# Holding expert weights back, rearranging the filling chain and adding filler matmuls in a fused attention and expert-routing kernel

## The chip, the cores and the metric

The kernel runs on one core of one Trainium2 chip. The metric is device time in microseconds of one execution, lower being better; the median of three runs of the kernel before is 372.67 us (371.42 to 376.82). The core has a matrix engine (TensorE, PE in the profile, with its weight loads as PEld), a vector engine (DVE), a scalar engine (ACT), GpSimd (POOL), a sync engine (SP) and 16 DMA engines that all queues share. Each engine takes its instructions in order and waits on semaphores.

## The reference

Two operators follow each other. The first is a linear attention with decay over q, k, v of shape (4, 8, 768, 64), in blocks of 64 positions; the second sends each of the 3072 resulting tokens (512 features) to one of eight experts, each with room for exactly 384 tokens, and applies that expert's two-layer network. The inputs are float32. Cut to what matters:

```python
for b in range(nb):                                  # blocks of one sequence
    intra = einsum('bhic,bhjc->bhij', qb, kb) * Dmask
    intra = einsum('bhij,bhjd->bhid', intra, vb)
    inter = einsum('bhid,bhde->bhie', qb * lam_pow, kv_state)
    out[:, :, sl] = intra + inter
    kv_state = lam_block * kv_state + einsum('bhsd,bhse->bhde', kb_dec, vb)

x = attn_out.transpose(0, 2, 1, 3).reshape(3072, 512)
logits = x @ w_gate                                  # 3072 x 8
order = argsort(-logits.flatten())                   # greedy, best pair first
for idx in order:
    tok, e = idx // E, idx % E
    if assigned[tok] >= 0 or counts[e] >= cap: continue    # cap = 384
    assigned[tok] = e; counts[e] += 1
for e in range(E):
    h = maximum(x[assigned == e] @ w1[e], 0.0)       # 512 -> 1024
    out[assigned == e] = h @ w2[e]                   # 1024 -> 512
```

The routing is sequential in the reference: an expert that fills up sends its later candidates to their next choice. The kernel finds the point at which each expert fills by counting.

## The kernel before

**Attention** (`_Attn`, run at L1070). 24 groups of 128 tokens pass through a software pipeline. In step s the loop loads group s + 3 (L909: q, k and v, 256 KB each, on SP's queue), turns q and k of group s + 1 on PE, applies the scores of group s - 1 to its values, computes the router's logits of group s - 2 (`gate`, L1055, whose copy at L1068 fills `logits[:, s - 2]`), computes the scores of group s (ACT and DVE split them into two bf16 parts, POOL masks them with an affine select at L979), and stores the attention output of group s - 1 to `x_dram` (L1043, 256 KB, on SP's queue). After that `hook(s)` runs, which also issues router constants, the ranges of the logits and the loads of expert weights 0 to 3 in steps 21 to 24 (L1136). A weight is one of sixteen matrices, w1 and w2 of eight experts in turn, read as float32 and written as bf16, 1 MB in SBUF. Load m is `load_w(m)` at L530, on POOL's queue. Weights 0 to 9 have their own room from the start. This part of the program is ordered on each engine by the framework's planner, which takes instructions as their inputs become ready and not strictly as they are written.

**Routing and experts** (`_route_and_moe`, L612). From here the order on PE, POOL and DVE is the written one. `router.phase1` is a generator. Its `first` (L200) settles the expert that fills first: three rounds, each of 24 matmuls that count tokens above thresholds (L222; the first at L228 and L230), a comparison and a one-matmul sum (`settle`, L205). Then it computes the positions of that expert's tokens and of the tokens that are first choices, builds one-hot matrices and, in 24 matmuls (L286), the token numbers `perm0` of the first two experts' first 256 tokens. 24 more matmuls (`psC`, L303) compact the tokens that are left over into 5 columns. Six filling steps (`steps`, L364) follow; each has three rounds of 5 counting matmuls (L388), one summing matmul (L404) and DVE work between them. In the first round of the first step `rest` (L328) also computes `R24`, `psT` (24 matmuls, L339) and with it `perm1`, the first 256 tokens of all experts. `perm2`, the last 128 tokens of each expert, comes after step 6.

Sixteen expert jobs run on PE: jobs 0 to 7 take 256 tokens of each expert, jobs 8 to 15 the last 128. A job gathers rows of `x_dram` by token number (L550, on POOL's queue, 128 rows at a time), turns them (L564), multiplies by w1 (`up`, L581), applies the maximum on ACT (L586), multiplies by w2 (`down`, L594), copies the result on ACT (L599, four buffers `oe`) and scatters it by token number to the output (L600, on POOL's queue). The filling steps are woven into the jobs' matmuls: a small planner keeps an estimate t of PE's time, each piece of a job adds its cost, and a filling step yields the delay in `WAIT` (L474) after which its next matmuls are to be put into PE's order. Loads 4 to 8 are written behind `moe.open` (L1141), load 9 behind the first gathers that need `perm1` (L668), and after the `up` of each job two more loads (L645), ahead of that job's two scatters.

## Time and profile before

| what | value |
|---|---|
| median of three runs | 372.67 us (371.42 to 376.82) |
| the profiled execution's own time | 374.97 us |
| its span, first to last instruction | 373.2 us |
| mean granted clock of PE | 0.82 |
| busy: PE, DVE, ACT, POOL | 268.0, 185.6, 168.2, 161.6 us |
| DMA queue of POOL / of SP and others by hardware | 26.22 MB, 37.7% / 25.19 MB, 31.9% of 16 engines' span |
| result scatters (L600) | 24, first issued at 242.5 us, last at 365.3 us |

Times in the profile are microseconds from the start of the span, unless marked ns. A line of the timeline names start, length, engine, source line, operation, output and inputs, and in brackets how long the engine sat idle before it and what released it. A release that names an engine long done hides another wait, often a DMA. SPq and POOLq are the queues' own entries: DMA issues and waits on semaphores. In the waits, columns are total, number of times and the longest. A DMA share above 1 means that packets on one engine overlap. The granted clock is a share of PE's full speed.

### The profile page before, as it was taken

What the parts mean: (1) busy time and instruction counts of PE and PEld (TensorE: products, weight loads), DVE (VectorE), ACT (ScalarE), POOL (GpSimd) and SP (SyncE); (2) the same over time, 40 slices, a digit from 0 to 9 for tenths busy, and PEclk for the clock granted to TensorE, in tenths of its full rate; (3) what the DMA queues carried; (4) which work ended last, traced back from release to release, by engine and by line L of the source; (5) the groups of instructions that cost most, each with busy time, mean ns of one, the idle gap of its engine ahead of it and who ended that gap; (6) DMA issues with size and microseconds to landing.
All of it is one profiled execution on the core that took longest, in us unless ns stands there. A gap on an engine that the chain in (4) does not pass through costs nothing. (4 is left out here: it accounts for less than half of the span.)

```text
span 373.2 us, 8812 instructions
## 1 busy us (share of the span) xinstructions
PE 268.0 (72%) x3551; PEld 210.7 (56%) x3551; DVE 185.6 (50%) x587; ACT 168.2 (45%) x297; POOL 161.6 (43%) x189
## 2 busy tenths in 40 slices
PE   2778455649588887988885556999939099786990
PEld 2567344528477786877764444666725067453760
DVE  3666505236467887788977655576716043000000
ACT  4655405345476786777620001444421236452650
POOL 5976322516355656557326044216060352535521
PEclk9998865685689899899965555799978679996997
DMA  8999999999996886874110042995939442414421
GB/s 155 218 181 213 216 218 212 177 209 218 220 224 156 189 205 145 190 175 112 61 53 5 2 56 33 188 205 104 205 73 186 99 102 82 100 59 117 95 86 35
DMA packets 96976, 52.05 MB, mean 139 GB/s; under 512 B 76960, under 2 KB 88224, under 8 KB 96928
## 3 DMA queue, kind: packets, MB, share of 16 engines
q0 software_dynamic: 17920, 26.22, 37.7%
q1 hardware_dynamic: 79008, 25.19, 31.9%
q8 instruction: 30, 0.49, 0.5%
q14 instruction: 18, 0.15, 0.1%
HBM read 58.74 MB, written 12.58 MB: 191 GB/s over the span
## 5 line engine op out<-in xcount | busy, mean ns | idle before, releaser
L581 PE MATMUL p<-xeT,w 128*128 128x256 bf16 (+1 forms) x512 | 53.9, 262 | 17.7 <-ACT hT L586 16.4
L600 POOL DMA_INDIRECT out_dram<-oe,perm x24 | 24.3, 1014 | 81.0 <-ACT oe L599 49.6
L581 PEld LDWEIGHTS <-w 128*128 128x128 bf16 x512 | 42.0, 103 | 27.6 <-issue 19.3
L979 POOL TENSOR_SCALAR_AFFINE_SELECT sp<-sp 128x512 f32<-128x512 f32 x48 | 30.7, 646 | 61.7 <-DVE sp L976 57.6
L594 PE MATMUL p<-w,hT 128*128 128x512 bf16 x192 | 47.5, 392 | 0.0
L975 ACT CAST sp<-S 128x512 bf16<-128x512 f32 x48 | 32.2, 738 | 22.0 <-PE S L970 21.9
L586 ACT ACTIVATE hT<-p 128x512 bf16<-128x512 f32 (+1 forms) x64 | 31.1, 491 | 22.4 <-PE p L581 16.6
L976 DVE TENSOR_TENSOR sp<-S,sp 128x512 bf16<-128x512 f32 x48 | 32.9, 734 | 15.4 <-ACT sp L975 15.2
L1010 PE MATMUL XL<-vh,sp 128*128 128x64 bf16 x384 | 27.7, 208 | 12.8 <-POOL sp L979 12.5
L550 POOL DMA_INDIRECT xe<-x_dram,perm x24 | 25.2, 1050 | 25.2 <-DVE B L294 11.2
L599 ACT COPY oe<-p 128x512 f32<-128x512 f32 x24 | 14.1, 586 | 46.2 <-DMA out_dram<-oe,perm 22.8
L933 POOL TENSOR_TENSOR vl<-vs,vh 128x512 bf16<-128x512 f32 x24 | 28.6, 1192 | 13.4 <-ACT vh L931 13.1
L1010 PEld LDWEIGHTS <-sp 128*128 128x128 bf16 x576 | 24.5, 108 | 16.3 <-POOL sp L979 14.9
L928 POOL TENSOR_TENSOR vs<-vf,lamneg 128x512 f32<-128x512 f32 x24 | 25.8, 1074 | 17.0 <-DMA vf<-in_v_dram 13.3
L568 ACT COPY xeT<-pt 128x1024 bf16<-128x1024 bf16 (+1 forms) x16 | 12.8, 798 | 42.9 <-PE pt L564 42.7
L925 ACT CAST kp<-kf 128x512 f16<-128x512 f32 x24 | 18.9, 789 | 27.6 <-DMA kf<-in_k_dram 27.6
L926 DVE TENSOR_TENSOR kp<-kf,kp 128x512 f16<-128x512 f32 x24 | 19.6, 816 | 23.4 <-ACT kp L925 23.4
L970 PE MATMUL S<-qh,kT 64*128 64x128 f16 x384 | 30.1, 239 | 1.2 <-DVE sp L976 1.1
L942 PE MATMUL kT_ps<-identf,kp 128*128 128x128 f32 x96 | 19.3, 338 | 15.8 <-DVE kp L926 11.0
L594 PEld LDWEIGHTS <-hT 128*128 128x128 bf16 x192 | 17.7, 100 | 17.9 <-issue 1.8
L970 PEld LDWEIGHTS <-kT 64*128 64x128 f16 x576 | 20.9, 104 | 10.3 <-issue 6.9
L1029 PE MATMUL stp<-vh,kp 128*128 128x128 bf16 x160 | 22.0, 252 | 4.7 <-ACT vh L931 3.9
(257 smaller groups left out, 592.7 us busy)
## 6 DMA issues: line engine op xcount, KB each, us to landing
w<-in_moe_w_dram POOLq DMA_DIRECT2D x16, 1024.0 KB
qf<-in_q_dram SPq DMA_DIRECT2D x24, 256.0 KB, 4.6
kf<-in_k_dram SPq DMA_DIRECT2D x24, 256.0 KB, 5.2
vf<-in_v_dram SPq DMA_DIRECT2D x24, 256.0 KB, 5.3
x_dram<-xs SPq DMA_DIRECT2D x24, 256.0 KB, 2.8
xe<-x_dram,perm POOLq DMA_INDIRECT x24
out_dram<-oe,perm POOLq DMA_INDIRECT x24
lam_sb<-in_lam_dram SPq DMA_DIRECT2D x1, 4.0 KB, 2.6
```

The costliest lines, as they stand in the source:

```text
L550: nc.gpsimd.indirect_dma_start(out=xe[:, c, :], out_offset=None, in_=self.x_dram, in_offset=bass.IndirectOffsetOnAxis(ap=pm, axis=0), boun ...
L581: nc.tensor.matmul(p1[:, f, 0:n, :], self.w1t[e][:, kc, fc * P : (fc + 1) * P], j["xeT"][:, kc, 0:n, :], start=(kc == 0), stop=(kc == 3), ...
L586: nc.scalar.activation(hT[:, fp, :, 0:n, :], p1[:, :, 0:n, :], ACT.Relu)
L594: nc.tensor.matmul(p2, j["hT"][:, kc // 2, kc % 2, c, :], self.w2t[e][:, kc, :], start=(kc == 0), stop=(kc == 7))
L600: nc.gpsimd.indirect_dma_start(out=self.out, out_offset=bass.IndirectOffsetOnAxis(ap=j["perms"][c], axis=0), in_=oe, in_offset=None, bound ...
L928: nc.gpsimd.tensor_tensor(vs, vf, self.lamneg[:, t, :, None].to_broadcast([P, 8, 64]), OP.mult)
L933: nc.gpsimd.tensor_tensor(vl, vs, vh, OP.subtract)
L970: nc.tensor.matmul(S[a][:, hp, :], kT[r, hp, :, ks], qq[r, hp, :], start=(i == 0), stop=(i == 2))
L975: nc.scalar.copy(s[:, :, :, 1], S[a])
L976: nc.vector.tensor_tensor(s[:, :, :, 0], S[a], s[:, :, :, 1], OP.subtract)
L979: nc.gpsimd.affine_select(out=sf, in_=sf, compare_op=OP.is_ge, fill=0.0, base=0, pattern=[[0, 4], [1, P]], channel_multiplier=-1)
L1010: nc.tensor.matmul(X[a][:, hp, :], sp[a][:, hp, :, ss], vv[:, h, :], start=(first and hp == 0 and i == 0), stop=(i == 2), skip_group_check ...
```

## The change

Seven edits, in the words of the code:

- `load_w` takes `after`: it first copies one logit on DVE into the first element of the weight tile, which the load then overwrites. Loads 0 to 6 are issued in steps 18 to 24 with the logits of group s - 2; loads 7 and 8 stay behind `moe.open` and have no such copy.
- Load 9 follows the first gathers, loads 10 and 11 follow the gathers of jobs 2 and 3 once `perm1` is there, and each later job issues one load ahead of its first scatter and one behind it. Gathers run four jobs ahead instead of three.
- `R24`, `psT` and `tok1` move from `rest` into `first`, behind `psC`.
- The filling step keeps the expert scores of dead tokens and masks the maximum instead; what the next step does not need at once moves behind its first indicators (`settled`).
- `warm(us)` issues `int(us / 0.11)` matmuls of 256 columns into an unused PSUM tile; it is called in `settle`, in `count`, before the last count of the first round, before `perm0`'s matmuls and before `psC`.
- `WAIT` has other values; the third, used once, goes from 1.5 to 5.5.
- `phase1` is given the tile for `warm`.

```diff
         G.tensor_tensor(self.zp[:, :, 1, a:b], Z, H, OP.add)
-    def phase1(self, ctx, L):
+    def warm(self, us):
+        for _ in range(int(us / 0.11) if self.spare is not None else 0):
+            self.nc.tensor.matmul(self.spare, self.identb,
+                                  self.i_kt.rearrange("p k t -> p (k t)")[:, 0:256],
+                                  start=True, stop=True)
+    def phase1(self, ctx, L, spare=None):
         tc = self.tc
...
         self.ps = ps
+        self.spare = spare
         self.sp2 = ctx.enter_context(tc.tile_pool(name="r2", bufs=2))
...
             nps = ps.tile([P, 8], F32, tag="n")
+            self.warm(0.25)
             nc.tensor.matmul(nps, onesm, S, start=True, stop=True)
...
                                 self.i_kt[:, 0:64, ts], OP.is_ge)
+                self.warm((0.9, 0.35)[hh])
                 for t in range(hh * 12, hh * 12 + 12):
...
         self.ranks(L, 23, 24)
+        self.warm(0.6)
         nc.tensor.matmul(cps, self.ind23, ohb[:, 23, :], start=False, stop=True)
...
         pe1 = ps.tile([P, 2, 6], F32, tag="n")
+        self.warm(3.0)
         for t in range(24):
...
         psC = ps.tile([P, 18, 5], F32, tag="pos")
+        self.warm(1.2)
         for t in range(24):
...
                              start=(t == 0), stop=(t == 23))
+        R24 = sp.tile([P, 2, 24, 24], F16, name="R24")
+        V.tensor_tensor(R24[:, 1], self.i_j[:, 0:24, :],
+                        jb[:, None, :].to_broadcast([P, 24, 24]), OP.is_equal)
+        V.tensor_tensor(R24[:, 0], R24[:, 1], self.i_t, OP.mult)
+        V.tensor_scalar(R24[:, 1], R24[:, 1], self.i_p, None, OP.mult)
         c1 = st.tile([P, 8], F32, name="c1")
...
         self.nf, self.big = nf, big
+        psT = ps.tile([P, 2, 24], F32, tag="cnt")
+        for t in range(24):
+            nc.tensor.matmul(psT.rearrange("p a j -> p (a j)"), A[:, :, t],
+                             R24[:, :, :, t].rearrange("p a j -> p (a j)"),
+                             start=(t == 0), stop=(t == 23))
         Z = st.tile([P, 8, 5], F32, name="Z")
...
         self.occ, self.alive = occ, alive
+        tok1 = st.tile([P, 8, 3], F32, name="tok1")
+        V.reduce_sum(tok1.rearrange("p e j -> p (e j)"), psT.rearrange("p a j -> p j a"), axis=AX.X)
+        self.tok1 = tok1
         def rest():
...
             self.tp = tp
-            R24 = sp.tile([P, 3, 24, 24], F16, tag="R", name="R24")
-            V.tensor_tensor(R24[:, 2], self.i_j[:, 0:24, :],
-                            jb[:, None, :].to_broadcast([P, 24, 24]), OP.is_equal)
-            V.tensor_tensor(R24[:, 0], R24[:, 2], self.i_t, OP.mult)
-            V.tensor_scalar(R24[:, 1], R24[:, 2], self.i_p, None, OP.mult)
-            psT = ps.tile([P, 2, 24], F32, tag="pos")
-            for t in range(24):
-                nc.tensor.matmul(psT.rearrange("p a j -> p (a j)"), A[:, :, t],
-                                 R24[:, 0:2, :, t].rearrange("p a j -> p (a j)"),
-                                 start=(t == 0), stop=(t == 23))
-            tok1 = st.tile([P, 8, 3], F32, name="tok1")
-            V.reduce_sum(tok1.rearrange("p e j -> p (e j)"), psT.rearrange("p a j -> p j a"),
-                         axis=AX.X)
-            self.tok1 = tok1
             perm1 = st.tile([P, 8, 3], I32, name="perm1")
...
         Z, alive, nf, big = self.Z, self.alive, self.nf, self.big
-        eoh = ge = oh = None
+        zr = nm = nps = am = oh = None
+        def settled(zr, nm, nps, am):
+            eoh = sp.tile([P, 8], F32, tag="eoh")
+            V.tensor_scalar(eoh, nps, nm, None, OP.is_equal)
+            V.scalar_tensor_tensor(big, eoh, 1.0e6, big, OP.mult, OP.add)
+            ge = sp.tile([P, 5], F32, tag="ge")
+            V.tensor_scalar(ge, zr, nm, None, OP.is_ge)
+            ga = sp.tile([P, 5], F32, tag="ga")
+            V.tensor_tensor(ga, ge, am, OP.mult)
+            V.tensor_tensor(self.aoi, self.aoi, ga, OP.add)
+            return ge
         for i in range(1, 7):
+            zm = sp.tile([P, 5], F32, tag="zm")
+            V.reduce_max(zm, Z, axis=AX.X)
             z = sp.tile([P, 5], F32, tag="z")
-            V.reduce_max(z, Z, axis=AX.X)
+            V.tensor_tensor(z, zm, alive, OP.mult)
             poh, oh = oh, sp.tile([P, 5, 8], BF16, tag="oh")
-            V.tensor_tensor(oh, Z, z[:, :, None].to_broadcast([P, 5, 8]), OP.is_equal)
-            zr = z
+            pzr, pnm, pnps, pam, zr = zr, nm, nps, am, z
             for r in range(3):
...
                     V.tensor_scalar(ind[:, c, :], self.kvec[r], zr[:, c : c + 1], None, OP.is_le)
+                if r == 0:
+                    V.tensor_tensor(oh, Z, zm[:, :, None].to_broadcast([P, 5, 8]), OP.is_equal)
                 if r == 0 and i > 1:
+                    ge = settled(pzr, pnm, pnps, pam)
                     ao = sp.tile([P, 5, 8], BF16, tag="ao")
...
                     yield rest()
+            V.scalar_tensor_tensor(nf, nps, nm, nf, OP.not_equal, OP.mult)
             V.scalar_tensor_tensor(alive, zr, nm, alive, OP.is_lt, OP.mult)
-            eoh = sp.tile([P, 8], F32, tag="eoh")
-            V.tensor_scalar(eoh, nps, nm, None, OP.is_equal)
-            V.tensor_tensor(nf, nf, eoh, OP.subtract)
             if i < 6:
-                V.tensor_tensor(Z, Z, alive[:, :, None].to_broadcast([P, 5, 8]), OP.mult)
                 V.tensor_tensor(Z, Z, nf[:, None, :].to_broadcast([P, 5, 8]), OP.mult)
-            V.scalar_tensor_tensor(big, eoh, 1.0e6, big, OP.mult, OP.add)
-            ge = sp.tile([P, 5], F32, tag="ge")
-            V.tensor_scalar(ge, zr, nm, None, OP.is_ge)
-            ga = sp.tile([P, 5], F32, tag="ga")
-            V.scalar_tensor_tensor(ga, zr, nm, am, OP.is_ge, OP.mult)
-            V.tensor_tensor(self.aoi, self.aoi, ga, OP.add)
+        ge = settled(zr, nm, nps, am)
         ef = sp.tile([P, 1], F32, tag="ef")
...
         yield perm2
-    WAIT = (1.5, 2.5, 1.5, 0.55, 2.2, 1.6)
+    WAIT = (1.4, 2.3, 5.5, 0.35, 2.2, 1.6)
     def flag(self):
...
             self.w2t[e] = pool.tile([128, 8, 512], BF16, name=f"w2_{e}")
-    def load_w(self, m):
+    def load_w(self, m, after=None):
         e = m // 2
-        if m % 2 == 0:
-            self.nc.gpsimd.dma_start(out=self.w1t[e], in_=self.w1r[e])
-        else:
-            self.nc.gpsimd.dma_start(out=self.w2t[e], in_=self.w2r[e])
+        w, src = (self.w2t[e], self.w2r[e]) if m % 2 else (self.w1t[e], self.w1r[e])
+        if after is not None:
+            self.nc.vector.tensor_copy(w[0:1, 0, 0:1], after)
+        self.nc.gpsimd.dma_start(out=w, in_=src)
     def open(self, ctx):
...
         self.mps = ctx.enter_context(tc.tile_pool(name="mps", bufs=2, space=bass.MemoryType.PSUM))
+    def spare(self):
+        return self.mps.tile([128, 256], F32, tag="p1", name="spare")
     def gather(self, perms):
...
     with tc.manual_schedule(engines={E.PE, E.Pool, E.DVE}):
-        gen = router.phase1(ctx, L)
+        gen = router.phase1(ctx, L, moe.spare())
         jobs = [None] * 16
...
         later = list(later)
+        moe.load_w(later.pop(0))
         perm1 = perm2 = None
...
                     yield from moe.turn(jobs[n + 1])
-                if jobs[min(n + 3, 15)] is None:
-                    ahead(n + 3)
-                for _ in range(2):
-                    if later:
-                        moe.load_w(later.pop(0))
+                if jobs[min(n + 4, 15)] is None:
+                    ahead(n + 4)
+                if later:
+                    moe.load_w(later.pop(0))
                 for c in range(len(jobs[n]["perms"])):
                     yield from moe.down(jobs[n], n % 8, c)
+                    if later and c == 0:
+                        moe.load_w(later.pop(0))
         ex = experts()
...
                     perm1 = got
-                    ahead(2)
-                    moe.load_w(later.pop(0))
+                    for n in (2, 3):
+                        ahead(n)
+                    for _ in range(2):
+                        moe.load_w(later.pop(0))
                 else:
                     perm2 = got
-                    for n in (8, 9, 10):
+                    for n in (8, 9, 10, 11):
                         ahead(n)
...
                 router.ranks(logits, 20, 23)
-            if 21 <= s <= 24:
-                moe.load_w(s - 21)
+            if 18 <= s <= 24:
+                moe.load_w(s - 18, logits[0:1, s - 2, 0:1])
         attn.run(hook)
     moe.open(ctx)
-    for m in range(4, 9):
+    for m in range(7, 9):
         moe.load_w(m)
...
```

## The prediction

> **What bounds the kernel now.** I read the page's slices first. The DMA row stands at 8 or 9 for the first quarter of the span and beyond, while the clock row falls to 5 there, and both look different further right.
>
> ```profile
> span 373.2 us, 8812 instructions
> PEclk9998865685689899899965555799978679996997
> DMA  8999999999996886874110042995939442414421
> ```
>
> Then busy time by stretch (columns: length, PE, PEld, DVE, ACT and POOL busy, granted clock, DMA share, GB/s). I cut the attention where step 3, step 9 and step 20 store their x tile.
>
> ```profile
> 32.60:101.20 68.60, 40.81 (x609) 34.54 (x608) 27.09 (x48) 27.57 (x47) 25.28 (x30) 0.68 1.12 211
> 101.20:166.10 64.90, 55.25 (x1102) 49.96 (x1096) 50.00 (x89) 48.06 (x86) 37.57 (x45) 0.92 0.84 185
> 245.00:250.00 5.00, 5.00 (x49) 3.58 (x47) 3.91 (x25) 2.72 (x5) 0.00 (x0) 1.00 1.22 207
> ```
>
> The timeline shows the stores of steps 3, 9 and 20, and the first and last of nine weight loads on POOL ahead of 100 us.
>
> ```profile
> 32.57 4.01 SPq L1043 DMA_DIRECT2D x_dram<-xs  x1
> 101.22 0.51 SPq L1043 DMA_DIRECT2D x_dram<-xs  x1
> 166.09 0.34 SPq L1043 DMA_DIRECT2D x_dram<-xs  x1
> ...
> 19.30 1.00 POOL L533 DMA_DIRECT2D w<-in_moe_w_dram  x1
> ...
> 86.66 0.82 POOL L533 DMA_DIRECT2D w<-in_moe_w_dram  x1
> ```
>
> Six steps took 101.22 - 32.57 = 68.65 us, 11.4 each; the next eleven took 64.87 us, 5.90 each. The slow stretch moves 211 GB/s at a DMA share of 1.12 with DVE and ACT busy less than half the time: it is bound by transfers. The code loads the first weights in steps 21 to 24, but the loads depend on nothing and the planner has pulled them to 19 to 87 us. The waits say the same; first 22.1 to 101.2 us, then 101.2 to 166.1 us:
>
> ```profile
> ACT kp L925 <- DMA kf<-in_k_dram: 24.8, 6, 11.1
> POOL vs L928 <- DMA vf<-in_v_dram: 13.3, 4, 5.7
> ...
> POOL sp L979 <- DVE sp L976: 25.7, 11, 4.3
> ```
>
> So once the weights are in, the pace is that of the chain ACT, DVE, POOL, PE over the score tiles.
>
> After attention the end is set by POOL's queue: every result scatter (L600) waits in it.
>
> ```profile
> L600 POOLq EVENT_SEMAPHORE  x24: 17/630/16816, 231.0 to 360.4; - x24
> 242.53 1.07 POOL L600 DMA_INDIRECT out_dram<-oe,perm  x1 [6.60 <-ACT oe L599]
> 243.54 0.59 ACT L599 COPY oe<-p 128x512 f32<-128x512 f32 x1 [1.29 <-PE p L594]
> 252.99 1.03 POOL L600 DMA_INDIRECT out_dram<-oe,perm  x1 [9.40 <-ACT oe L599]
> 279.06 1.06 POOL L600 DMA_INDIRECT out_dram<-oe,perm  x1 [0.30 <-issue]
> 294.30 1.03 POOL L600 DMA_INDIRECT out_dram<-oe,perm  x1 [14.19 <-ACT oe L599]
> 298.32 1.03 POOL L600 DMA_INDIRECT out_dram<-oe,perm  x1 [0.30 <-ACT hT L586]
> ...
> 314.46 0.99 POOL L600 DMA_INDIRECT out_dram<-oe,perm  x1 [3.46 <-ACT oe L599]
> 317.99 0.98 POOL L600 DMA_INDIRECT out_dram<-oe,perm  x1 [2.53 <-ACT hT L586]
> ...
> 365.31 0.98 POOL L600 DMA_INDIRECT out_dram<-oe,perm  x1 [3.75 <-ACTq L696]
> ```
>
> These are scatters 1, 2, 5, 6, 7, 11, 12 and 24 of 24, all into one tensor. The second has its tile (the ACT copy) at 244.1 us but is issued at 252.99: I read this as each scatter waiting until the one before has landed. Scatters 1 and 5 stand behind weights in the same queue and hold their successor 10.5 and 15.2 us. Without weights, 298.32 to 365.31 is 17 intervals of 3.94 us.
>
> **Part one: weights held (L530, L1136).** Seven loads now wait, through a copy of one logit into the weight tile, for the logits of steps 16 to 22. Loads 7 and 8 have no such copy; I take them to go to 19 and 22 us. Up to 32.57 us nothing then differs. Steps 3 to 9 run at 5.90: 6 x 5.90 = 35.4 for 68.65, a gain of 33.3 us. The cost is at steps 18 to 24. POOL issues seven more loads there and stands on the score chain; the load also waits for the copy on DVE, with POOL's affine selects queued behind it and PE behind those. I take half of an issue of 0.82 (the row at 86.66) each, 7 x 0.41 = 3 us. Nothing is the lower bound. For the upper: a weight is 1.05 MB, at 207 GB/s 5.1 us, a step's own loads and store another 1.05 MB, 5.0 us at 211; in the three steps that still load inputs, 10.1 stands against 5.90, which is 12.6 us. I take the low value because loads are issued nearly two steps, 11.8 us, ahead.
>
> ```profile
> DMA to landing us min/median/max: 3.8/5.2/21.1
> ```
>
> This is the landing time of the kf loads: 5.2 us in the median, at worst 21.1. [...]
>
> The last logits, at 197.60 now, come at 197.6 - 33.3 + 3 = 167.3 us. I call that point L.
>
> **Part two: the routing.**
>
> ```profile
> 197.60 0.22 DVE L1068 COPY logits<-Lo 128x8 f32<-128x8 f32 x1
> 212.54 1.88 PE L286 MATMUL pe<-B1v,ind 128*128 128x12 f16 x24 [3.35 <-DVE B1v L281]
> 214.46 0.17 DVE L289 TENSOR_REDUCE perm<-pe 128x6 int32<-128x12 f32 x1 [1.11 <-PE pe L286]
> 216.37 4.11 PE L303 MATMUL psC<-R,ind 128*128 128x90 f16 x24 [1.95 <-DVE R L300]
> 218.66 0.99 POOL L550 DMA_INDIRECT xe<-x_dram,perm  x1 [0.30 <-issue]
> 220.52 0.20 DVE L318 COPY zl<-psC 128x40 f32<-128x40 f32 x1 [3.72 <-issue]
> 222.15 0.84 PE L388 MATMUL cps<-oh,ind 128*128 128x8 bf16 x5 [1.67 <-DVE ind L380]
> 223.79 0.16 DVE L330 COPY tp<-psC 128x10 f32<-128x10 f32 x1
> 225.15 2.36 PE L339 MATMUL psT<-R,ind 128*128 128x48 f16 x24 [1.73 <-DVE R L336]
> 227.55 0.21 DVE L343 TENSOR_REDUCE tok<-psT 128x24 f32<-128x48 f32 x1 [2.46 <-PE psT L339]
> 227.79 0.18 DVE L347 CAST perm<-tok 128x24 int32<-128x24 f32 x1
> 232.76 1.86 PE L581 MATMUL p<-xeT,w 128*128 128x256 bf16 x8
> 245.24 1.91 PE L581 MATMUL p<-xeT,w 128*128 128x256 bf16 x16
> 197.60:214.50 16.90, 9.40 (x104) 7.83 (x103) 10.79 (x41) 0.00 (x0) 5.73 (x8) 0.50 0.00 1
> ```
>
> R24 and psT leave the stretch from tp to perm1: 227.79 - 223.79 = 4.0 us. They come back ahead of the first count: psT, 2.36 us on PE, covered by DVE's 1.63 us between zl and the count, so 0.7, and a reduction of 0.2. Net -3.1. If that cover went (clock as before, DVE late), at most the 4.0 would come back.
>
> The fillers: int(us / 0.11) gives 2 in each of three settles, 8 + 3 in each of two counts, 5, 27 and 10: 70 matmuls of 256 columns, 0.12 us each at full clock (1.91 / 16), 0.23 at half (1.86 / 8), 8 or 16 us of PE in a stretch where PE has 16.9 - 9.4 = 7.5 us idle before perm0. At full clock they fit the gaps and cost nothing; the longest, 27 x 0.12 = 3.2, fits the 3.35 us ahead of pe1. At half clock they overfill the count gaps by about 1 us each and the gap before pe1 by some 3 us: +4. Does the clock rise? It is 0.50 here with PE 56% busy on matmuls of 8 columns. Full clock would halve PE's share on the path; I put it at 4 to 5 us before perm1, mostly psC, which takes 4.11 us. Ends -5 and +4; the last gate stretch is thin, so I expect the clock to start low and rise on the way, and take -2.
>
> [...]
>
> Perm1, at L + 30.2 now, comes at L + 25; perm0, L + 16.9 now, at L + 16. The deferred DVE operations of each filling step, the other WAIT values and the gathers four ahead I cost at nothing: expert matmuls lie beside them, and PE has slack against POOL's queue.
>
> ```profile
> 298.30:365.30 67.00, 57.34 (x523) 38.96 (x522) 7.89 (x52) 32.41 (x67) 27.41 (x27) 0.91 0.35 90
> ```
>
> PE is idle for 9.7 of 67 us there. Should PE now stand 0.2 us, the cut in WAIT between count and settle, in each of the 18 rounds, that is 3.6 us, still inside it; without that cover it would be 3.6 us on the end.
>
> **Part three: the queue after L.** Weights 0 to 6 and the stores leave about 14 us of transfers at L (seven weights at 5.1, three steps' loads at 3.7 and eight stores at 1.2 make 56.4 us of work, begun at step 18, two steps before 166.09, 43 us before L), done before the first gathers at L + 17. These are four issues of 0.99 + 0.30, then load 9 goes at L + 22. From there the one queue carries, up to scatter 5: weights 9 to 15 (7.34 MB), ten gathers of 128 x 512 bf16, 0.13, four scatters of as many f32, 0.26: 9.70 MB, at 207 GB/s 47 us, and 2.5 us for a scatter to land (the wait at 317.99): L + 72. Now it is 279.06 - 197.60 = L + 81.5. This takes the queue as never empty, which holds because load 13 goes behind scatter 1 and load 15 behind scatter 3 rather than two loads ahead of a pair.
>
> From scatter 5 on no weights are left. 19 intervals x 3.94 = 74.9, and 373.2 - 365.31 = 7.9 to the end: 82.8 for 94.1 now. Interval bounds: 3.53 (314.46 to 317.99), 7.8 us less; 94.1 as now.
>
> **Sum.** 167.3 + 72 + 82.8 = 322.1 us of span, 51 less. The profiled execution took 374.97, 1.8 over its span, so 323.9; the median 372.67 is 2.3 lower: 322.
>
> **The rivals.**
> *The queue gives part back.* Scatters stay behind weights as now: scatter 5 at L + 76, then 94.1: 337 span, 337. For: one queue, the 15.2 us wait. Against: fewer loads in front. 0.17.
> *All goes well.* No price at steps 18 to 24, full clock (-3), 3.53 us intervals: 164.3 + 69 + 75.0 = 308. For: rows for each. Against: three at once. 0.15.
> *The fillers do not lift the clock.* +4 instead of -2 in the routing, which reaches the queue through load 9: 328. For: 0.50 today with PE 56% busy. Against: 256 columns each stream far longer than 8. [...] 0.08.
> *The hold does not hold*, and the nine loads go early again: attention ends at 197.6, the rest as forecast: 352. Against: the copy makes a real dependency. 0.06.
> *Slower: POOL stands still.* POOL works in order. If held loads are placed a step too early, each stops POOL, and with it the affine selects (25.7 us of waits are around them already), for a step of 5.90 and slows the next by 4.2 of shared transfers: 7 x 10.1 = 71 instead of 3, 390. It ends over 2% slower from (380 - 322 + 3) / 7 = 8.7 us a load. For: in-order queue. Against: the planner places by readiness. 0.04.
>
> **How the numbers follow.** The forecast has 0.50, its own range 312 to 331. To hold 8 in 10 the range takes in the good case and the first and third rival with some margin: 304 to 341. Two per cent is about 7.5 us, what a measurement can tell. Slower 0.03, same 0.02 (a mild form of the POOL stop), faster 0.95.
>
> **What would show it.** Steps 3 to 9 at 5.9 us each, DMA share below 1 there; seven loads after 115 us; L near 167; granted clock above 0.50 in the 25 us after L, perm1 near L + 25; scatter 5 near L + 72; then 3.5 to 4 us a scatter. Wrong if kf or POOL waits appear in steps 18 to 24 for over 10 us, if PE waits for filler matmuls ahead of a count, or if a scatter after the fifth still waits over 6 us.

## The result and the profile after

The changed kernel takes 332.79 us in the median of four runs (332.27 to 334.09), the kernel before, run beside it, 374.02 (371.42 to 376.82): a ratio of 0.890, 95% interval 0.883 to 0.898. Run again beside the last experiments it took 327.85 us (324.94 to 332.49), a ratio of 0.877 (0.866 to 0.889); what the two profiles show of these 5 us is told below. The forecast was 322 with a range of 304 to 341. The range holds the time; the point lies 11 us too low for the first measurement and 6 for the second. The narrower 312 to 331, which the prediction gave to its main case, holds only the second.

The page of the changed kernel, its head and the rows for the granted clock and the DMA share in 40 slices:

```profile
span 330.4 us, 8960 instructions
...
PEclk9999899999997999795558967999978999999985
DMA  8999999789696899999894089999984215234210
```

The clock row no longer falls in the second and third tenth of the span, and the empty DMA slices in the middle have shrunk to one. Busy time by stretch, cut at the same events as for the kernel before (columns as there: length, five engines, granted clock, DMA share, GB/s):

```profile
33.47:65.40 31.93, 28.32 (x585) 24.46 (x580) 25.86 (x44) 24.60 (x44) 18.56 (x21) 0.96 0.99 220
65.41:128.27 62.86, 54.16 (x1118) 47.38 (x1112) 51.58 (x93) 50.18 (x89) 38.87 (x46) 0.97 0.87 190
128.27:167.20 38.93, 27.61 (x502) 23.65 (x503) 27.98 (x86) 16.58 (x29) 18.86 (x23) 0.72 1.05 197
167.20:186.30 19.10, 17.89 (x166) 14.33 (x166) 10.80 (x41) 0.00 (x0) 5.51 (x8) 0.77 0.60 113
197.40:246.50 49.10, 37.74 (x338) 26.07 (x338) 31.19 (x180) 19.22 (x30) 19.72 (x20) 0.92 1.10 193
246.50:322.30 75.80, 62.98 (x596) 43.55 (x595) 13.31 (x83) 37.10 (x75) 29.32 (x30) 0.95 0.31 85
```

The first row is steps 3 to 9, which took 68.65 us before; the third is step 20 to the last logits (point L), 31.5 us before (197.60 - 166.09). The fourth, L to perm0, is longer than the 16.9 us of before, although its clock is 0.77 and not 0.50. The timeline of the changed kernel, with what DVE, PE and POOL do after L:

```profile
167.23 0.23 DVE L1097 COPY logits<-Lo 128x8 f32<-128x8 f32 x1
186.28 0.17 DVE L301 TENSOR_REDUCE perm<-pe 128x6 int32<-128x12 f32 x1 [1.58 <-PE pe L298]
188.19 4.14 PE L316 MATMUL psC<-R,ind 128*128 128x90 f16 x24 [0.84 <-DVE R L312]
192.88 0.97 POOL L557 DMA_DIRECT2D w<-in_moe_w_dram  x1
197.43 0.17 DVE L359 CAST perm<-tok 128x24 int32<-128x24 f32 x1
208.48 1.05 POOL L625 DMA_INDIRECT out_dram<-oe,perm  x1 [0.30 <-issue]
...
225.82 1.03 POOL L625 DMA_INDIRECT out_dram<-oe,perm  x1 [15.35 <-ACT oe L624]
...
246.50 1.03 POOL L625 DMA_INDIRECT out_dram<-oe,perm  x1 [3.15 <-ACT oe L624]
250.09 1.00 POOL L625 DMA_INDIRECT out_dram<-oe,perm  x1 [2.56 <-ACT hT L611]
...
322.28 0.99 POOL L625 DMA_INDIRECT out_dram<-oe,perm  x1 [2.52 <-DMA out_dram<-oe,perm]
```

These are L, perm0, psC, load 9, perm1 and scatters 1, 2, 5, 6 and 24. Scatter 1 still has weights ahead of it and holds scatter 2 for 15.35 us. Scatter 5 is followed by scatter 6 after 3.6 us; before it took 15.2.

All runs in one table, L and the four stretches behind it from each run's profile (us):

| kernel | median (lowest to highest) | L | to perm0 | to perm1 | L to scatter 5 | scatter 5 to end |
|---|---|---|---|---|---|---|
| before | 374.02 (371.42 to 376.82) | 197.6 | 16.9 | 30.2 | 81.5 | 94.1 |
| changed | 332.79 (332.27 to 334.09) | 167.2 | 19.1 | 30.2 | 79.3 | 83.9 |
| changed, again | 327.85 (324.94 to 332.49) | 162.0 | 20.6 | 31.7 | 82.4 | 81.6 |
| before, hold alone | 345.87 (344.59 to 346.96) | 167.2 | 16.9 | 30.3 | 82.2 | 93.5 |
| changed, no hold | 362.17 (357.28 to 366.45) | 199.8 | 19.9 | 31.1 | 80.6 | 84.2 |
| changed, old load order | 348.15 (345.22 to 352.22) | 170.6 | 19.3 | 30.4 | 84.7 | 95.2 |
| changed, no fillers | 326.40 (322.89 to 331.06) | 161.0 | 16.9 | 28.0 | 77.1 | 83.1 |
| changed, late hold | 326.55 (325.49 to 328.28) | 161.7 | 19.0 | 30.2 | 79.6 | 82.5 |
| changed, psC side by side | 336.51 (332.99 to 341.98) | 166.8 | 20.6 | 38.3 | 86.5 | 83.9 |
| changed, two targets | 318.47 (316.41 to 320.73) | 160.9 | 20.6 | 31.7 | 74.3 | 79.9 |
| no fillers, late hold | 324.08 (321.88 to 328.06) | 160.6 | 16.7 | 27.9 | 77.2 | 82.5 |
| the same, load 9 in step 12 | 324.82 (323.46 to 325.22) | 163.5 | 16.8 | 28.0 | 76.8 | 82.7 |
| the same, loads 9, 10 at perm0 | 322.81 (321.13 to 323.75) | 161.6 | 16.8 | 27.9 | 76.6 | 83.8 |
| both | 321.64 (320.25 to 323.61) | 162.0 | 16.8 | 28.0 | 73.1 | 84.0 |

The profiles without the hold, with the old load order and with psC side by side are of slow executions (366.45, 352.22 and 338.87 us), so their stretches can be a few per cent longer than in the median run.

### The profile page after: what moved, and what is told of

Its sections match the earlier page's. It is cut to its first block, busy times and chain, and to the rows that moved or that the text cites. A ratio compares the mean times of both kernels' runs of the same rounds, so it can differ in the third digit from the quotient of the medians.

```text
span 330.4 us, 8960 instructions
## 1 busy us (share of the span) xinstructions
PE 258.1 (78%) x3621; PEld 203.4 (62%) x3621; DVE 187.8 (57%) x595; ACT 167.0 (51%) x297; POOL 163.4 (49%) x189
## 5 line engine op out<-in xcount | busy, mean ns | idle before, releaser
L606 PE MATMUL p<-xeT,w 128*128 128x256 bf16 (+1 forms) x512 | 51.4, 256 | 11.4 <-ACT hT L611 7.4
L1008 POOL TENSOR_SCALAR_AFFINE_SELECT sp<-sp 128x512 f32<-128x512 f32 x48 | 31.5, 665 | 34.1 <-DVE sp L1005 33.1
L619 PE MATMUL p<-w,hT 128*128 128x512 bf16 x192 | 45.9, 379 | 0.0
L1004 ACT CAST sp<-S 128x512 bf16<-128x512 f32 x48 | 32.4, 744 | 19.1 <-PE S L999 18.9
L957 POOL TENSOR_TENSOR vs<-vf,lamneg 128x512 f32<-128x512 f32 x24 | 27.0, 1126 | 15.1 <-DMA vf<-in_v_dram 11.5
L999 PE MATMUL S<-qh,kT 64*128 64x128 f16 x384 | 28.5, 227 | 1.5 <-DVE sp L1005 1.2
L619 PEld LDWEIGHTS <-hT 128*128 128x128 bf16 x192 | 16.9, 97 | 18.8 <-issue 2.2
L1039 PE MATMUL XL<-vh,sp 128*128 128x64 bf16 x384 | 24.7, 200 | 4.4 <-POOL sp L1008 3.8
L1039 PEld LDWEIGHTS <-sp 128*128 128x128 bf16 x576 | 21.7, 102 | 7.6 <-POOL sp L1008 6.9
L999 PEld LDWEIGHTS <-kT 64*128 64x128 f16 x576 | 19.3, 98 | 6.7 <-issue 4.0
L1039 PE MATMUL XL<-vl,sp 128*128 128x64 bf16 x192 | 22.4, 199 | 0.0
L982 PE MATMUL qT_ps<-identf,qf 128*128 128x128 f32 x96 | 17.7, 311 | 5.2 <-POOL i_kt L42 5.2
L999 PE MATMUL S<-ql,kT 64*128 64x128 f16 x192 | 21.8, 226 | 0.0
```

The lines of the kernel that those rows point to most:

```text
L606: nc.tensor.matmul(p1[:, f, 0:n, :], self.w1t[e][:, kc, fc * P : (fc + 1) * P], j["xeT"][:, kc, 0:n, :], start=(kc == 0), stop=(kc == 3), ...
L619: nc.tensor.matmul(p2, j["hT"][:, kc // 2, kc % 2, c, :], self.w2t[e][:, kc, :], start=(kc == 0), stop=(kc == 7))
L957: nc.gpsimd.tensor_tensor(vs, vf, self.lamneg[:, t, :, None].to_broadcast([P, 8, 64]), OP.mult)
L999: nc.tensor.matmul(S[a][:, hp, :], kT[r, hp, :, ks], qq[r, hp, :], start=(i == 0), stop=(i == 2))
L1004: nc.scalar.copy(s[:, :, :, 1], S[a])
L1008: nc.gpsimd.affine_select(out=sf, in_=sf, compare_op=OP.is_ge, fill=0.0, base=0, pattern=[[0, 4], [1, P]], channel_multiplier=-1)
```

## The experiments

My theory after the result: the hold brings some 28 to 30 us in attention, the new order of loads and scatters some 10 to 15 behind it, and the routing nothing, because the fillers take what the shorter chain gives. The rivals: that the hold gives part of its gain back behind L; that the loads' order matters little; that the fillers carry the clock of the experts; that something other than the landing of scatters, that is the arrival of their data in the output, sets their pace.

### The hold alone, and all but the hold

The kernel before, with the held loads and nothing else (its `load_w` takes `after` as in the change):

```diff
-            if 21 <= s <= 24:
-                moe.load_w(s - 21)
+            if 18 <= s <= 24:
+                moe.load_w(s - 18, logits[0:1, s - 2, 0:1])
...
-    for m in range(4, 9):
+    for m in range(7, 9):
```

> The kernel before with the held weights alone: seven loads wait for the logits of steps 16 to 22, the rest of the routing, the fillers' absence and the order of loads and scatters as before. Theory A (the hold is worth what attention loses less, and the queue order is worth the rest): L comes at 167 us as in the changed kernel, L to scatter 5 stays at 81 to 84 us, scatter 5 to the end stays at 94 us: 343 to 347 us, of which some 10 to 14 us are left to the other parts. Rival B (the hold only works with the new order): the backlog of weights at L stands in front of the gathers, scatter 5 comes at L + 90 or later and the time is 352 us or more. Rival C (the hold does all): 335 us or less.

The changed kernel, with the same lines turned back:

```diff
-            if 18 <= s <= 24:
-                moe.load_w(s - 18, logits[0:1, s - 2, 0:1])
+            if 21 <= s <= 24:
+                moe.load_w(s - 21)
...
-    for m in range(7, 9):
+    for m in range(4, 9):
```

> The changed kernel with its weights loaded as before the change: nothing holds them. Theory A (the parts add up): L comes at 197 us again and the rest takes what it takes in the changed kernel, 163 us: 361 to 363 us. Rival B (part of the gain is given back, because held weights are still in flight at L): L to scatter 5 is shorter than 79.3 us, at 72 to 75, since no weights are left at L, and the time is 354 to 357 us. My record gave 352 us for this case.

The hold alone took 345.87 us, a ratio of 0.931 (0.921 to 0.942) to before; all but the hold 362.17, 0.966 (0.947 to 0.985). The timeline of the kernel with the hold alone, L and scatters 5 and 6:

```profile
167.16 0.22 DVE L1070 COPY logits<-Lo 128x8 f32<-128x8 f32 x1
...
249.38 1.05 POOL L602 DMA_INDIRECT out_dram<-oe,perm  x1 [0.30 <-issue]
263.89 1.03 POOL L602 DMA_INDIRECT out_dram<-oe,perm  x1 [13.46 <-ACT oe L601]
```

L is where the changed kernel has it, and behind L everything is as in the kernel before: 82.2 and 93.5 us for 81.5 and 94.1, with the wait of 13 us between scatters 5 and 6. So the hold is worth 374 - 346 = 28 us, and the weights that are still in flight at L cost under 1 us there. Without them the changed kernel has scatter 5 at L + 80.6, no earlier than the 79.3 with them; but that profile is of the longest of four runs, and the shortest, 357.28 us, comes close to the 354 to 357 of rival B and has no profile. So it is mainly the kernel with the hold alone that speaks against the rival that the hold gives part of its gain back.

### The old order of loads

```diff
-        moe.load_w(later.pop(0))                 # behind the first gathers
...
-                if later:
-                    moe.load_w(later.pop(0))
+                for _ in range(2):
+                    if later:
+                        moe.load_w(later.pop(0))
                 for c in range(len(jobs[n]["perms"])):
                     yield from moe.down(jobs[n], n % 8, c)
-                    if later and c == 0:
-                        moe.load_w(later.pop(0))
...
-                    for _ in range(2):           # behind the gathers of perm1
-                        moe.load_w(later.pop(0))
+                    moe.load_w(later.pop(0))
```

> The changed kernel, with loads 9 to 15 put where the kernel before has them: none behind the first gathers, one behind perm1's, two ahead of each of the first three jobs' scatters. Theory A (a scatter that stands behind weights holds its successor until both have landed, and the last pair then falls into the run of scatters): scatter 5 or 6 waits over 10 us again, scatter 5 to the end takes 92 to 94 us for 83.9, and the time is 341 to 345 us. Rival B (the loads' place in the queue matters little, the transfers are the same bytes; what shortened the run of scatters is something else in the change): 331 to 335 us.

It took 348.15 us, 0.936 (0.927 to 0.945) of before, 15 and 20 more than the two measurements of the changed kernel. Its timeline, two loads and scatters 5 and 6:

```profile
253.20 1.76 POOL L557 DMA_DIRECT2D w<-in_moe_w_dram  x2
255.26 1.05 POOL L625 DMA_INDIRECT out_dram<-oe,perm  x1 [0.30 <-issue]
269.31 1.03 POOL L625 DMA_INDIRECT out_dram<-oe,perm  x1 [12.99 <-ACT oe L624]
```

The wait of 13 us is back, behind two loads that stand directly ahead of scatter 5. Scatter 5 to the end takes 95.2 us for 83.9, and scatter 5 itself comes 5.4 us later after L (2.3 against the second profile of the changed kernel). Theory A holds, with a time 3 us above its range. With this the gain has its parts: 28 us from the hold, about 15 from the order of loads, and from the rest (chain and fillers together) nothing: this kernel has hold, chain and fillers, and its median is 2 us above that of the hold alone, with ranges that overlap. Taken off in the other order, all parts but the hold are worth 374 - 362 = 12 us together, close to 15 - 2.

### No filler matmuls

```diff
-        for _ in range(int(us / 0.11) if self.spare is not None else 0):
+        for _ in range(0):
```

> The changed kernel without any of its filler matmuls. Theory A (the fillers only stand in the way of the counts): each of the three counts settles some 1 us earlier, the first gathers and everything behind them in POOL's queue move up by about 2.2 us: L to perm0 16.9 us as before the change, not 19.05; granted clock 0.50 from L to the first expert matmul; the time about 330.5 us against 332.8. The count matmuls keep their pace (24 for psC in about 4.1 us) although the clock is lower there. Rival B (the fillers carry the clock): the expert matmuls start colder, psC takes longer, scatter 5 comes later than L + 79 and the time is 335 to 338 us.

326.40 us, 0.878 (0.862 to 0.895) of before. The timeline and a window of this kernel:

```profile
160.96 0.22 DVE L1097 COPY logits<-Lo 128x8 f32<-128x8 f32 x1
172.34 0.21 PE L273 MATMUL cps<-cum,ones 128*128 128x9 bf16 x1
175.91 1.88 PE L298 MATMUL pe<-B1v,ind 128*128 128x12 f16 x24 [3.35 <-DVE B1v L292]
177.82 0.17 DVE L301 TENSOR_REDUCE perm<-pe 128x6 int32<-128x12 f32 x1 [1.10 <-PE pe L298]
179.74 4.14 PE L316 MATMUL psC<-R,ind 128*128 128x90 f16 x24 [1.95 <-DVE R L312]
```

```profile
179.70:183.90 4.20, 4.17 (x27) 3.83 (x28) 1.62 (x7) 0.00 (x0) 3.29 (x4) 0.50 0.50 63
```

The way from L to perm0 is 16.9 us again, perm1 comes at L + 28.0 and scatter 5 at L + 77.1, each 2.2 us earlier than with fillers. psC takes 4.14 us at a granted clock of 0.50; with the fillers it took 4.14 at 1.00, as the next window of the changed kernel shows, here with its rows of `cps`, of the longest filler group and of `pe`:

```profile
180.33 0.21 PE L273 MATMUL cps<-cum,ones 128*128 128x9 bf16 x1
180.40 4.22 PE L193 MATMUL spare<-i_kt,identb 128*128 128x256 bf16 x27
184.46 1.78 PE L298 MATMUL pe<-B1v,ind 128*128 128x12 f16 x24
...
188.20:192.50 4.30, 4.30 (x28) 3.97 (x29) 1.70 (x8) 0.00 (x0) 3.39 (x4) 1.00 0.54 66
```

So the fillers do raise the clock, and the work they raise it for hardly runs faster: psC not at all, the 24 matmuls of `pe` in 1.78 us for 1.88. The 2.2 us are lost in two places. `cps`, the matmul ahead of the longest group, starts at L + 11.4 without fillers and at L + 13.1 with them, so 1.7 us go in the counts; the longest group then adds 0.6. From scatter 5 to the end it is 83.1 us for 83.9, so the experts don't miss them either: theory A. Of the 9.2 us between the two profiled spans (330.4 and 321.2) the fillers explain 2.2, and 0.8 in the tail at most; the rest is L, which is 6.3 us earlier here although nothing ahead of L was edited. The medians do not price the fillers: 326.40 is 1.5 us under the second measurement of the changed kernel, and the ranges overlap.

### The hold three steps later

```diff
-            if 18 <= s <= 24:
-                moe.load_w(s - 18, logits[0:1, s - 2, 0:1])
+            for m, at in enumerate((21, 21, 22, 22, 23, 23, 24)):
+                if s == at:
+                    moe.load_w(m, logits[0:1, s - 2, 0:1])
```

> The changed kernel with the seven held loads at steps 21, 21, 22, 22, 23, 23 and 24, when the last q, k and v loads have been issued, not one each at steps 18 to 24. Theory A (the 7.5 us that steps 20 to the end of attention take more than before come from weights that delay the last v tiles): the wait of 6.3 us for vf goes, L comes 4 to 7 us earlier, at 160 to 163 us. If POOL's queue after L can take the backlog, the time falls as much, to 326 to 329 us. Rival B (the backlog moves behind L): 7 weights at 5.1 us begin some 20 us before L and end up to 16 us behind it, so the first gathers land late and scatter 5 comes later than L + 79 by what L gained: 333 us, no change, or up to 338. Rival C (POOL's issues, not transfers, cost the 7.5 us): L stays at 167.

326.55 us (325.49 to 328.28), 0.880 (0.869 to 0.891) of before; L at 161.65, and 79.6 and 82.5 us behind it: theory A. The two long waits for transfers ahead of L in the changed kernel, from its waits between 116 and 172 us (columns: total, times, longest); they overlap in time, one ending at 151.0 us and the other at 152.5:

```profile
POOL vs L957 <- DMA vf<-in_v_dram: 6.6, 2, 6.3
DVE xs L1044 <- DMA x_dram<-xs: 5.2, 1, 5.2
```

And the same line in the second profile of the changed kernel, where L came at 161.99:

```profile
POOL vs L957 <- DMA vf<-in_v_dram: 0.9, 2, 0.5
```

The last v tile is on time in one execution and 6 us late in another. Of the seven profiles with held loads from step 18, four have L at 166.8 to 170.6 (in the latest it is a k tile that ACT waits for, 8.7 us) and three at 160.9 to 162.0; of the five with held loads from step 21, all have it at 160.6 to 163.5. In all four late ones the wait for an input tile is 5.7 to 8.7 us, in the others at most 0.7. That fits the reading that weights delay the tile, and the runs of the late hold spread by 2.8 us only. Five profiles don't prove that it can't happen there. The kernel with the hold alone has the late tile too (6.8 us), so its 28 us are with that wait included.

### psC's operand side by side

```diff
-        R5 = sp.tile([P, 18, 5, 24], F16, tag="R", name="R5")
+        R5c = sp.tile([P, 24, 18, 5], F16, tag="R", name="R5")
+        R5 = R5c.rearrange("p t n j -> p n j t")
...
-                             R5[:, :, :, t].rearrange("p n j -> p (n j)"),
+                             R5c[:, t].rearrange("p n j -> p (n j)"),
```

> The changed kernel, with psC's 90 moving columns laid side by side in memory, not 48 bytes apart; the same numbers are computed, VectorE writes them in the other order. Theory A (the stride of the operand sets the pace of these matmuls, whatever clock is granted): psC takes 1.7 to 2.2 us for its 24 matmuls, not 4.14, with the clock no higher than in the changed kernel; VectorE may lose 0.5 to 1 us on its writes; zl and perm1 come 1 to 2 us earlier, and of the time at most 2 us go, 331 to 333, since the first loads and gathers stand behind perm0. Rival B (the clock sets the pace): psC stays at 4.1 us.

336.51 us, 0.900 (0.891 to 0.908) of before. Its timeline and the window of psC:

```profile
187.74 9.05 DVE L310 TENSOR_TENSOR R<-B,r_zp 128x1920 f16<-128x1920 f16 x1
188.34 8.95 POOL L576 DMA_INDIRECT xe<-x_dram,perm  x1 [15.14 <-DVE B L307]
197.95 2.02 PE L317 MATMUL psC<-R,ind 128*128 128x90 f16 x24 [9.54 <-DVE R L313]
```

```profile
197.90:199.90 2.00, 1.95 (x26) 1.96 (x27) 1.63 (x7) 0.00 (x0) 1.69 (x2) 0.50 0.65 80
```

psC takes 2.02 us at a clock of 0.50, half of the 4.14 that it takes at 0.50 and at 1.00 with its columns 48 bytes apart. Theory A is right on the matmuls and far off on the price: DVE's write in the other order takes 9.05 us, not 1.16 and half or one more, and the first gather on POOL, beside it, 8.95 instead of 1.59. In the changed kernel these are:

```profile
186.68 1.16 DVE L309 TENSOR_TENSOR R<-B,r_zp 128x1920 f16<-128x1920 f16 x1
187.28 1.59 POOL L575 DMA_INDIRECT xe<-x_dram,perm  x1 [13.59 <-DVE B L306]
```

Whether the write's stride, 180 bytes between neighbours, alone makes the 9.05, or the gather beside it has a share, wasn't tried.

### Every second scatter to another tensor

```diff
+        dst = self.out if self.n_out % 2 == 0 else self.out2
+        self.n_out += 1
         nc.gpsimd.indirect_dma_start(
-            out=self.out, out_offset=...
+            out=dst, out_offset=...
```

> The changed kernel, with every second scatter of results written to a scratch tensor in place of the output, so half of the output's rows are left out. Two scatters that follow each other then have no tensor in common. Theory A (each scatter waits until the one before has landed, some 3.5 us, and that is what the run of scatters costs): the scatters no longer wait for each other; from scatter 5 to the end PE becomes the bound, with 63 us busy, so 83.9 falls to 70 to 76 and the time is 319 to 325 us. Rival B (the scatters come at the pace at which PE makes the tiles, or at which POOL issues): 331 to 334 us.

The second tensor is a scratch one, so this kernel leaves half of the output's rows out. 318.47 us, 0.859 (0.851 to 0.867) of before. Scatters 1, 2, 17 and 18 of its timeline, and its last stretch:

```profile
203.65 1.05 POOL L628 DMA_INDIRECT out_dram<-oe,perm  x1 [0.30 <-issue]
205.94 1.03 POOL L628 DMA_INDIRECT out<-oe,perm  x1 [0.30 <-ACT hT L612]
...
279.43 1.01 POOL L628 DMA_INDIRECT out_dram<-oe,perm  x1 [3.03 <-ACT hT L612]
283.39 1.02 POOL L628 DMA_INDIRECT out<-oe,perm  x1 [1.62 <-ACT oe L625]
```

```profile
270.00:307.00 37.00, 34.56 (x368) 24.03 (x366) 0.15 (x1) 21.89 (x51) 13.11 (x13) 1.00 0.30 86
```

Scatter 2 follows scatter 1 after 2.3 us where it took 17.3: a scatter waits for its predecessor into the same tensor, as I had read it from the kernel before. But the gain sits elsewhere than I wrote. Of the 15.3 us between the first profile of the changed kernel and this one, 6.3 are an earlier L, which the edit does not touch. Scatter 5 comes at L + 74.3, 5 us earlier than in the first profile of the changed kernel, and the run behind it takes 79.9 us, not 70 to 76: from scatter 17 on all but the last come 3.96 to 3.99 us apart, with PE busy 93% at full clock. One scatter up to its landing (3.5 us: in the changed kernel the last went at 322.28 us, after 2.52 us of waiting for the one before it, issued at 318.77) and PE's work on one 128-token job (4.0) lie so close that freeing the one uncovers the other.

### The parts put together

The two repairs together, then one and two moved loads on top of them. First, the edits of the kernel without fillers and of the late hold in one:

```diff
+        for _ in range(0):
...
+            for m, at in enumerate((21, 21, 22, 22, 23, 23, 24)):
```

> The changed kernel without filler matmuls and with the held loads at steps 21, 21, 22, 22, 23, 23 and 24. Theory A (the two costs are separate and add): L at 160 to 163 us in every run, perm0 at L + 16.9, scatter 5 at L + 77.3, the end 83 later: 323 to 325 us. Rival B (leaving the fillers out was worth 6 us by itself and the late loads another 6): 319 to 321 us. Rival C (both remove the same 6 us): 326 to 327 us.

324.08 us (321.88 to 328.06), 0.872 (0.865 to 0.880). The stretches are those of theory A: L at 160.6, perm0 at L + 16.7, scatter 5 at L + 77.2, the end 82.5 later. The time lies in its range too, but the ranges of this kernel and of each repair alone overlap, so the times don't tell it from rival C.

Then, with it, load 9 in step 12:

```diff
+            if s == 12:
+                moe.load_w(9, logits[0:1, s - 2, 0:1])
...
-    fi = _route_and_moe(ctx, tc, logits, router, moe, range(9, 16))
+    fi = _route_and_moe(ctx, tc, logits, router, moe, range(10, 16))
```

> No filler matmuls, the seven held loads at steps 21 to 24, and load 9 held to the logits of step 10, so that it is carried in steps 12 to 14, where the DMA share is 0.87. Theory A (up to scatter 5 the one queue's bytes set the time): one weight less behind perm0, 5.1 us, so scatter 5 comes at L + 72 to 73 in place of L + 77, the attention loses 0 to 2 us, and the time is 319 to 321 us against 324 for the same kernel with load 9 behind perm0. Rival B (scatters wait for the expert matmuls, and those for the routing): L + 77 stays, 324 to 326 us.

324.82 us, 0.872 (0.864 to 0.880): the numbers of rival B, though not its reason, as the waits below show. Scatter 5 comes at L + 76.8, where one weight less should have brought L + 72. Scatters 3 to 4 in this kernel, and in the one with the load behind perm0:

```profile
225.90:236.30 10.40, 8.41 (x79) 5.84 (x79) 6.22 (x38) 3.67 (x6) 1.06 (x2) 1.00 0.79 132
```

```profile
222.00:232.30 10.30, 8.41 (x79) 5.84 (x79) 6.50 (x39) 3.66 (x6) 1.96 (x2) 1.00 1.11 199
```

The stretch lasts as long at 132 GB/s as at 199. Fewer bytes in the queue don't shorten it: in both kernels scatter 3 has a weight directly ahead of it, and scatter 4 waits 8 to 9 us although its tile was done 12 us before scatter 3 went. The load that is saved stood behind scatter 3: scatter 5 now follows scatter 4 after 4.0 us instead of 5.4, but scatter 2 follows scatter 1 after 17.7 instead of 16.9, for a reason that I did not find.

In its place, two loads behind perm0 and one behind perm1:

```diff
         later = list(later)
-        moe.load_w(later.pop(0))
+        for _ in range(2):
+            moe.load_w(later.pop(0))
...
-                    for _ in range(2):
-                        moe.load_w(later.pop(0))
+                    moe.load_w(later.pop(0))
```

> No filler matmuls, the seven held loads at steps 21 to 24, and load 10 right behind load 9 at perm0 in place of behind the gathers of perm1. Theory A (bytes of the queue): the 11 us from perm0 to perm1 stand at a DMA share of 0.59 now, 4.6 us idle; that fills, scatter 5 comes at L + 73 to 75, 320 to 322 us. Rival B (the gathers of perm1, now behind two weights, come too late for the third expert job): scatter 5 at L + 77 or later, 324 to 328 us.

322.81 us, 0.866 (0.858 to 0.874), 1.3 less than the same kernel with one load there; scatter 5 at L + 76.6, where theory A wanted 73 to 75. The ranges of the two overlap, so this is not told apart from no change.

Both of the last two edits:

> Both of these: load 9 in steps 12 to 14, and loads 10 and 11 behind perm0. Theory A: scatter 5 at L + 68 to 70, 315 to 318 us. From there the run of scatters, 3.5 us each, and PE stay as they are, 82 to 84 us. Rival B (something else than the queue holds the first scatters): 321 to 325 us.

321.64 us (320.25 to 323.61), 0.866 (0.857 to 0.875): scatter 5 at L + 73.1, 4 us earlier than without the two moves and not the 7 to 9 that I expected, the end 84.0 later. Of the 4 us, 2.3 lie between scatters 1 and 2 (14.6 for 16.9) and 1.4 between 4 and 5 (4.0 for 5.4). Each move alone brought scatter 5 forward by some 0.5 us or less; why the two together give more is open. Beside it, on the same chip:

> The changed kernel itself, beside the others: 331 to 334 us, L at 165 to 168, since its seven held loads begin at step 18 as before; if the late v tile is a matter of chance, one run in four some 6 us shorter, as without the fillers.

327.85 us (324.94 to 332.49): L at 162.0 in the one profile, and three of the four times are 324.94 to 327.92, so here the short run, which I take to be the one with the early v tile, was the rule and not one in four. The version with all four edits is 6.2 us faster than the changed kernel, and the ranges don't overlap; at 1.9% it lies near the limit of what such a measurement tells.

## Why the prediction was right, and where it was not

**The hold.** Steps 3 to 9 take 31.93 us, 5.3 a step, where I took 5.90 from the later steps: 3.5 us better than forecast. The DMA share there is 0.99, below 1 as I wrote but by a hair, and the clock and DVE are now at 0.96 and 81%. Steps 20 to L take 38.93 us in the first profile, 7.5 more than before, and 34.4 in the second (127.57 to 161.99), 2.9 more. My +3 for half of each issue fits the second in size, as does the late hold, whose 34.6 us hold no wait for an input tile; no run shows that it is the issues that cost it. The first has the late v tile, a risk for which I had a row (a kf landing of 21.1 us at worst) and the bound of 12.6. L came at 167.23 for a forecast of 167.3, which is luck, two misses that cancel: 3.5 us in steps 3 to 9 and 2.0 in steps 9 to 20 on one side, 0.9 by which step 3 comes later and 4.5 behind step 20 on the other.

The low value rested on the lead: input loads go out 11.8 us ahead, against a median landing of 5.2 us for the kf loads of the kernel before. That the lead would do beside held weights was my choice; no trace had shown it. In four of seven profiles it did not: a tile kept its engine waiting, for 6.3 us in the changed kernel's first, where the v tile landed 17.2 us after its issue. It had more than one weight beside it: three loads went out within 9.2 us (133.42, 139.43 and 142.58 us) for a tile issued at 133.73, and three weights at 5.1 us each, 1.05 MB at the 207 GB/s of before, are an estimated 15.3 us of transfers.

**The routing** is the step that failed. I had perm1 at L + 25; it came at L + 30.2, no earlier than before the change. Two terms were wrong.
- "Full clock would halve PE's share on the path, mostly psC." The clock came (1.00 through psC), the halving didn't. psC, the largest part of it, did not follow the clock but the layout of its operand: with columns 48 bytes apart it is 4.14 us at 0.50 and 4.14 at 1.00, and 2.02 at 0.50 once they lie side by side. The `pe` matmuls gain 0.1 us; what sets their pace was not tried.
- The fillers cost 2.2 us up to perm0 in the first profile, and up to 3.7 in others (L to perm0 is 19.0 to 20.6 in seven profiles with fillers and 16.7 to 16.9 in seven without). I had put -2, with +4 as the other end. Of the 2.2, 1.7 are lost in the counts and 0.6 at the longest group, 27 matmuls for which I had 3.2 us at full clock. It took 4.22 at a mean clock of 0.73, and 5.36 in the second profile, where perm0 comes at L + 20.6. That PE would wait for fillers ahead of a count was one of my signs of being wrong, and it came.

R24 and psT moved, as forecast, and gave 2.2 us instead of 3.1 (30.2 to 28.0 without fillers): the count now waits for psT, the reduction and what else lies ahead of it, so that from `zl` to `tp` it is 4.98 us for 3.27, 1.7 more where I had 0.9. The copy that makes `perm1` stayed in `rest`, behind the first round's DVE operations: its numbers are summed up at 194.75 us and it runs at 197.43. Up to 2.7 us were left lying there; no run moves that copy. The rival "the fillers do not lift the clock" gave the right sign for the wrong reason, and its 328 is 5 us from the first measurement and 0.2 from the second.

What sets the granted clock is not shown. That a busier PE is granted more was my estimate, from 0.50 at 56% busy between L and perm0; with the fillers PE is busy 94% of that stretch in the first profile and 96% in the second, and the clock is 0.77 and 0.64. The length of PE's gaps does not tell it either. In the kernel before, the granted clock falls from 1.00 (184 to 186 us) to 0.50 (187 to 190) although no gap of PE between 176 us and L is over 0.8 us. Without the fillers it stays at 0.50 from L to psC, with all gaps but one (3.35 us) shorter than 2 us; with the fillers between them it goes to 1.00 for parts.

**The queue after L.** Load 9 goes at L + 25.65, where I had 22 (perm0 3 us later, and 0.6 more behind it). From there to scatter 5 it is 53.6 us, for 47 + 2.5: the 193 GB/s of the stretch from perm1 on, instead of 207, make 50.3 + 2.5 of it, and the 187 GB/s of these 53.6 us themselves 51.9 + 2.5. So the sum, load 9 at L + 22 and 50 us from there, was short by 3.7 and 3.6. The step's reason, one queue that is never empty, is only half of it: with 1.05 MB taken out of the queue scatter 5 did not move, with both moves it came 4 us earlier. My reading is that what counts there is which scatters have a weight directly ahead of them: scatters 1 and 3 have one in all these kernels, and the long waits stand behind these two. No run took the weight away from one of them alone, so this is not shown. The weaker claim of the same part, that the order of loads and scatters frees the run behind scatter 5, is shown by the old order: 95.2 us against 83.9.

**The tail.** 19 intervals take 75.8 us, 3.99 each, for 3.94; the end is 8.1 us for 7.9. PE is busy 63 of the 75.8, which is the slack to which I left the shorter WAIT. The slack has run out where the jobs are 128 tokens: the kernel with two targets shows PE as the next bound, at 4.0 us a job.

**The whole.** 167.2 + 79.3 + 83.9 = 330.4 for 167.3 + 72 + 82.8 = 322.1: 7.3 of the 8.3 us that are missing lie between L and scatter 5. Of the 41 us that were gained, 28 are the hold, about 15 the order of loads, and -2 the chain with the fillers. On the stretch to scatter 5 the rival of the queue that gives part back was nearer: scatter 5 came later than its L + 76. Its other half, 94.1 us from there, did not come. The rivals of a hold that doesn't hold and of a POOL that stands still did not come: without the hold the time is 362, where I had written 352 with too much credit for the other parts.

## What to carry to other kernels

Before warming the clock for a row of short matmuls, ask what sets their pace: if the same matmuls take the same time at half and at full clock, as psC did here (4.14 us at 0.50 and at 1.00), fillers gain nothing on them, and the layout of the operand is the thing to look at (2.02 us side by side), with the price of writing it in the other order (9.05 us on DVE for 1.16). Loads that depend on nothing are issued when the planner likes; tie them to a result, late enough that they don't meet the last input tiles: with loads held from step 18 an engine waited 5.7 to 8.7 us for such a tile in four of seven profiles, with loads held from step 21 in none of five. In a queue that carries both weights and results that wait for each other, look not only at the bytes but at the results that stand directly behind a weight: with two loads ahead of scatter 5, scatter 6 came 14.05 us after it, with none 3.59.

## What the runs showed of the hardware that was not expected

- A matmul of 90 columns with 48 bytes between them takes 172 ns (4.14 us for 24) at a granted clock of 0.50 and of 1.00, and 84 ns (2.02 for 24) side by side at 0.50. No run tells what the other operand, the weights, 48 bytes apart too, adds.
- The same elementwise DVE operation over 1920 float16 elements a partition took 1.16 us with its output in order and 9.05 us with 180 bytes between neighbours, and a gather on POOL that started beside it 8.95 us for 1.59.
- The same kernel's last v tile, read while weights are in flight, was ready on time in some profiles and 6 us late in others. The two profiles of the changed kernel differ by that in L, 167.23 and 161.99; that its two medians, 332.79 and 327.85 us, differ for the same reason is likely and not shown, since each has one profile.
